# Attention and a feed-forward layer on one core: reciprocals and mixed tails go through the two PV banks

## The chip, the core and the metric

The kernel runs on one core of a Trainium2 chip. The metric is the device time of one execution in microseconds. Engines are named as in the profile: PE (TensorE), DVE (VectorE), ACT (ScalarE), POOL (GpSimd), SP (the DMA queue's engine).

## The reference, cut to what matters

```python
def _attn_ref(q, k, v, w1, b1, w2):          # q, k, v: (4, 8, 576, 64)
    scores = scale * np.matmul(q, k.transpose(0, 1, 3, 2))
    ...                                      # bias: a small network of relative positions
    scores = scores + bias.transpose(2, 0, 1)[None, :, :, :]
    scores = scores - np.max(scores, axis=-1, keepdims=True)
    attn = np.exp(scores)
    attn = attn / (np.sum(attn, axis=-1, keepdims=True) + 1e-09)
    return np.matmul(attn, v)

def _moe_ref(x, w_in, w_out):                # x: (2304, 512), d_ff = 2048
    h = x @ w_in
    g = np.maximum(0.01 * h, h)
    return g @ w_out
```

The output of attention, with heads side by side, is the x of the feed-forward layer.

## The kernel before, in words

Three parts follow each other. The bias is generated first (to about 49 us), then attention runs, then the feed-forward part (from 314.68 us). The order of all instructions is written out by hand, each engine runs its own in that order, and the framework only adds waits. It orders accesses of different engines to one PSUM bank of a tile.

Attention works on 16 units. A unit is a pair of heads of one batch entry. It has nine score tiles, in the order A0, B0, A1, B1, M, A2, B2, A3, B3 (`KINDS`). A and B are the two heads, 128 query rows each; M is the mixed tile, the last 64 rows of both heads. `step(n)` handles tile n of 144:

- `qk_mm(n)` (L242 for M, L249 for the others): the score product of tile n on PE, into a ring tile.
- `softmax_a(n)` (L272): the score read on DVE, which adds the bias, writes p and takes the row's extreme.
- `recip(n-1)` if that was M or B3 (L288, L289 on DVE, L292 and L294 on POOL): reciprocals of the row sums, spread to a tile rb.
- `pv_exit` for a PV group that is done (L363, DVE): the PV result times the transposed reciprocals (slot 8 of `PT`), into x.
- `transposes(n-3)` (PE, L305): tile n-3 is transposed into another ring tile by 64x64 blocks, 8 to 16 products, and copied to `PT` by ACT (L342, for M L326). For M the tails of the mixed tile, its reciprocals and those of group 0 go into the same ring tile, which DVE copies out in three more instructions (L329 twice, L312). For B3 the reciprocals of group 1 do so, copied by L312.
- `pv` (L357): PV products of the queue `pv_q` that are due. A unit has two groups: group 0 for the query rows of A0, B0, A1, B1 and half of M, group 1 for the rest. Each group has five parts c, of four PE instructions in the trace. Group 0 comes whole two steps after M's transposes, that is in the step of the next unit's A0. Group 1 comes two steps after B3's transposes (c = 0, 1, 2; M's step) and four steps after (c = 3, 4; B2's step).
- `softmax_b` (L280): exp on ACT.

In steps of A0, M and B3 two conversion instructions for the feed-forward weights follow on DVE (L417 to L423).

PSUM has eight banks. Ring tiles take six: two buffers `s` of two banks and one buffer `u` of two, in turn s, s, u (`sttile`). A step takes two ring tiles, first for the score product, then for the transposes; 18 turns make a unit, so each kind falls on the same tag in every unit. M's and A3's score products use u, and so do the transposes of B3, A1 and A2. M's transposes use s; that buffer is next used by the score product of the following A0. The buffer u with B3's transposes is next used by the score product of M. The last two banks are two buffers `o`, one for each PV group in turn.

Of the kernel before, what the change touches and what calls it, by code (L numbers as in the profile page):

```python
# [8 lines left out]
F32 = mybir.dt.float32  # L9
# [5 lines left out]
B, H, S, D, HID = 4, 8, 576, 64, 32  # L15
DM, DFF = 512, 2048
NT = B * S
HP = H // 2
# [19 lines left out]
LAG = 3  # L38
# [4 lines left out]
def attention_ffn(ctx: ExitStack, tc: tile.TileContext, qk_in, v_in, wi, wo, cst, out):  # L43
    nc = tc.nc
    PS = bass.MemoryType.PSUM
    xp = ctx.enter_context(tc.tile_pool(name="xp", bufs=1))
    ps = ctx.enter_context(tc.tile_pool(name="ps", bufs=2, space=PS))
    po = [ExitStack()]
# [12 lines left out]
    def po_open():  # L61
        po[0].close()
        po[1:] = [po[0].enter_context(tc.tile_pool(name="po", bufs=2, space=PS, reuse_waits="tile"))]

    def pstile(tag):
        shape = [128, 512] if tag in "to" else [128, 1024]
        return (ps if tag == "s" else po[1]).tile(shape, F32, tag=tag, name="ps_" + tag, bufs=1 if tag == "u" else 2)

    turns = [0]

# [10 lines left out]
    PT = ap.tile([128, 2, 10, HS], F32, name="PT")  # L81
# [170 lines left out]
    mx_t, sm_t, rb_t, pair = {}, {}, {}, [None]  # L252
# [43 lines left out]
    outs = {}  # L296
    pv_q = []

    def banks(t, a, b):
        return t[:].rearrange("p (r x) -> p r x", r=2)[:, :, a:b]  # L300

    def turn(dst, src):
        for r in range(2):
            q = slice(64 * r, 64 * r + 64)
            nc.tensor.transpose(dst[:, r, :], src[q, :], ident[q, q])  # L305

    def turn_rb(t, rb):
        for i in range(2):
            turn(t[:, :, 64 * i:64 * i + 64], rb[:, 128 * i:128 * i + 128])

    def copy_rb(u, g, t):
        nc.vector.tensor_copy(PT[:, g, 8, 0:256].rearrange("p (i r c) -> p i r c", i=2, r=2), t.rearrange("p r (i c) -> p i r c", i=2))  # L312

    def transposes(n, at):
        u, kind = tile_id(n)
        p = pp.pop(n)
        p0 = S + 64 if kind[0] == "B" else 0
        t0 = sttile()
        for jb in range(4):
            turn(banks(t0, 64 * jb, 64 * jb + 64), p[:, p0 + 128 * jb:p0 + 128 * jb + 128])  # L320
        if kind == "M":
            rb = rb_t.pop((u, 0))
            turn(banks(t0, 320, 384), p[:, 512:640])
            turn(banks(t0, 256, 320), rb[:, 256:384])
            turn_rb(banks(t0, 384, 512), rb)
            nc.scalar.copy(out=PT[:, :, 0:8, 256:288].rearrange("p g (j h) c -> p g j h c", h=2), in_=banks(t0, 0, 256).rearrange("p h (j g c) -> p g j h c", j=4, g=2))  # L326
            for h in range(2):
                r = slice(64 * h, 64 * h + 64)
                nc.vector.tensor_copy(PT[r, :, 8:10, 256:288], banks(t0, 256, 384)[r, h, :].rearrange("p (a g c) -> p g a c", a=2, g=2))  # L329
            copy_rb(u, 0, banks(t0, 384, 512))  # L330
            pv_q.extend((at, u, 0, c) for c in range(5))
            return
        ic, h = int(kind[1]), 0 if kind[0] == "A" else 1
        g, i2 = ic // 2, ic % 2
        c = slice(128 * i2, 128 * i2 + 128)
        nj = 4 + h
        if h == 1:
            turn(banks(t0, 256, 320), p[:, 512:640])
        if kind == "B3":
            turn_rb(banks(t0, 320, 448), rb_t.pop((u, 1)))  # L340
        dst = PT[:, g, :, c].rearrange("p (j h) c -> p j h c", h=2)[:, 0:nj, h, :]
        nc.scalar.copy(out=dst.rearrange("p j (r c) -> p j r c", r=2), in_=banks(t0, 0, 64 * nj).rearrange("p r (j c) -> p j r c", j=nj))  # L342
        if kind == "B3":
            copy_rb(u, 1, banks(t0, 320, 448))
            pv_q.extend((at + 2 * (c > 2), u, 1, c) for c in range(5))

    pv_out = []

    def pv():
        _, u, g, jb = pv_q.pop(0)  # L350
        hp, b = divmod(u, B)
        if jb == 0:
            outs[u, g] = pstile("s" if (u, g) == (HP * B - 1, 1) else "o")
        o, pt = outs[u, g], PT[:, g]
        for h in range(2):
            l, r = vv[u][:, jb, 64 * h:64 * h + 64], pt[:, 2 * jb + h if jb < 4 else 9, :]
            nc.tensor.matmul(o[64 * h:64 * h + 64, 0:HS], l, r, start=(jb == 0), stop=(jb == 4))  # L357
        if jb == 4:
            pv_out.append((hp, S * b + HS * g, o, pt[:, 8, :]))

    def pv_exit():
        hp, t0, o, r = pv_out.pop(0)
        nc.vector.tensor_mul(x1[hp][:, t0:t0 + HS], o[:, 0:HS], r)  # L363

    NTILE = 9 * HP * B

    def step(n):
        first = n == 7
        if first:
            transposes(n - LAG, n + 1)  # L370
        if n == 5:
            recip(n - 1)
        if 1 < n < NTILE:
            qk_mm(n)
            if n % 9 == 4 and n // 9 + 2 < HP * B:
                load_unit(n // 9 + 2)
            if 10 <= n < 10 + LATE:
                dst, e = late[n - 10]
                nc.sync.dma_start(out=dst, in_=e)
            softmax_a(n)  # L380
        if n != 5 and 0 <= n - 1 < NTILE and KINDS[(n - 1) % 9] in ("M", "B3"):
            recip(n - 1)
        while pv_out and n < NTILE + LAG + 2:
            pv_exit()
        if 0 <= n - LAG < NTILE and not first:
            transposes(n - LAG, n + 2)
        while pv_q and pv_q[0][0] <= n:
            pv()
        while ex_q and n != 5:
            softmax_b()  # L390
# [209 lines left out]
    with tc.manual_schedule():  # L600
# [6 lines left out]
        for n in range(NTILE + LAG + 6):  # L607
            u, i = divmod(n, 9)
            if u == 0:
                while done < GEN_AT[i]:  # L610
                    gen_tick(done)
                    done += 1
            if n == 9:
                gen.close()
                early = pools["early"] = ctx.enter_context(tc.tile_pool(name="early", bufs=1, side="right"))
                w1b[0] = w1b[1] = early.tile([128, 2, 7, 256], F32R, name="w1a")
                for m in range(EARLY + 1):
                    y2[m] = early.tile([128, DM], F32, name=f"y2_{m}")
                early.tile([128, 24], F32, name="gap")
                r_last = early.tile([128, 320], F32, name="r_last")  # L620
                for c in ("raw", "y1"):
                    pools[c] = ctx.enter_context(tc.tile_pool(name=c, bufs=1, side="right"))
            if n == 2:
                po_open()
            step(n)
            if n == 13:
                w_fill()
                early_ops = conversion(halves_[:NE])
                for g in range(PRE):
                    t = 9 * (4 + 3 * g)  # L630
                    extra[t + 1] = [(s_sum, g, 0)]
                    extra[t + 4] = [(s_sum, g, 1), (s_sum, g, 2)]
                    extra[t + 6] = [(w1_hi, g, 0, nc.gpsimd.tensor_copy)]
                    extra[t + 7] = [(w1_hi, g, 1)]
                    extra[t + 10] = [(s_sum, g, 3)]
                    extra[t + 12] = [(w1_hi, g, 3)]
                    extra[t + 13] = [(w1_lo, g, 0, nc.gpsimd), (w1_lo, g, 1, nc.gpsimd)]
                    extra[t + 15] = [(w1_hi, g, 4, nc.gpsimd.tensor_copy)]
                    extra[t + 17] = [(w1_out, g, 0)]
                    extra[t + 18] = [(w1_out, g, 1)]  # L640
                    extra[t + 19] = [(w1_lo, g, 3, nc.gpsimd)]
                    extra[t + 22] = [(w1_lo, g, 4, nc.gpsimd)]
                    extra[t + 24] = [(w1_out, g, 2)]
                    extra[t + 26] = [(w1_out, g, 3)]
                extra[9 * 14 + 4] = [(w1_in, 0)]
                for k, o in enumerate((3, 2, 4)):
                    extra[NTILE - 8 + (0, 1, 5)[k]] = [(x_sum, 0, o)]
            for f, *args in extra.get(n, ()):
                f(*args)
            left = {0: 2, 4: 2, 8: 2}.get(i, 0) if n >= 18 else 0  # L650
            while early_ops and left:
                f, *args = early_ops.pop(0)
                f(*args)
                left -= f == w_bits
            if u < HP * B:
                if u % B == B - 1 and u // B + 1 < HP:
                    c = {1: "0", 2: "1", 4: "2", 5: "M", 6: "3"}.get(i)
                    if c:
                        load_bias(u // B + 1, c)
                if i == 8 and u + 2 < HP * B:  # L660
                    load_v(u + 2)
# [194 lines left out]
```

## Time and profile before

| | us |
|---|---|
| median of three runs | 696.05 (695.57 to 696.22) |
| profiled execution | 696.33 |
| its span | 694.5 |

Shares of that span in which an engine was busy: PE 95%, PE's weight loads 72%, DVE 65%, ACT 60%, POOL 19%.

In the rows of the profile, a line such as L357 is that line of the kernel before; `PE ps_o L357` means PE writing the tile ps_o there. An idle time in brackets is the time in which the engine had nothing to run just ahead of the row, with what ended it by the trace. PE's instructions overlap: a group's duration runs to the end of its last one, and the next group can start before that, so the time that a group costs is read from start to start.

### The profile page before, as it was taken

Reading aid. Unit: us, or ns where it says so; the run is one execution under the profiler, and the core shown is the slowest. Engines: PE = TensorE matmul, PEld = TensorE weight load, DVE = VectorE, ACT = ScalarE, POOL = GpSimd, SP = SyncE. Lnnn points to the kernel's source line nnn. Section 1 sums busy time; section 2 is a strip of 40 time slices with the busy share of each in tenths; the row PEclk is TensorE's granted clock in tenths of the full one; section 3 lists DMA queues with packets and bytes.
Section 4 is the critical chain, followed back from the end, with each engine's and each line's share of the span. In section 5 each row is a group of like instructions: output and inputs, shape, how many; then the busy total and the mean of one; then the engine's idle time right before and its main releaser. Section 6 shows DMA issues by size and latency. Waiting matters only on the chain.

```text
span 694.5 us, 13060 instructions
## 1 busy us (share of the span) xinstructions
PE 657.4 (95%) x4990; PEld 498.5 (72%) x4990; DVE 454.7 (65%) x1041; ACT 417.6 (60%) x879; POOL 131.0 (19%) x177
## 2 busy tenths in 40 slices
PE   9987899989988999989999999999999999999997
PEld 5434555555555555558889889899889889898886
DVE  7994677776777777659899987534343663334343
ACT  8996788888888888777445546433333544333332
POOL 0000002322222220133000051221114421221110
PEclk9999999999999999999999999999999999999999
DMA  8989247447654783025256526452222244432302
GB/s 276 300 280 325 74 132 258 160 139 272 211 192 152 241 282 147 6 107 197 92 170 201 213 65 235 176 198 108 107 107 106 107 168 164 152 138 107 107 1 91
DMA packets 36542, 113.95 MB, mean 164 GB/s; under 512 B 7584, under 2 KB 12320, under 8 KB 34048
## 3 DMA queue, kind: packets, MB, share of 16 engines
q1 hardware_dynamic: 36272, 112.91, 47.7%
q8 instruction: 39, 0.64, 0.4%
q14 instruction: 23, 0.19, 0.1%
q10 hardware_dynamic: 208, 0.21, 0.1%
HBM read 82.59 MB, written 30.52 MB: 163 GB/s over the span
## 4 chain that ended last, share of the span: by engine, by line
PE 83%; ACT 10%; DVE 3%; issue 1%; DMA 1%; POOL 0%; POOLq 0%; ACTq 0%
PE ps_t L532 25%; PE ps_s L574 19%; PE ps_o L357 12%; PE ps_o L574 10%; PE ps_s L305 5%; ACT p L280 4%; ACT PT L342 4%; PE ps_s L249 3%; PE ps_u L249 3%; DVE p L272 2%; PE ps_u L242 2%; PE ps_o L145 1%; PE ps_t L145 1%; DVE PT L312 1%; PE ps_s L145 1%
## 5 line engine op out<-in xcount | busy, mean ns | idle before, releaser
L544 DVE TENSOR_TENSOR c<-ps_t,c 128x384 f32<-128x384 f32 x164 | 88.8, 555 | 128.9 <-PE ps_t L532 127.8
L551 ACT ACTIVATE g<-c 128x384 fp32r<-128x384 f32 x96 | 50.6, 527 | 179.7 <-DVE c L544 154.6
L574 PE MATMUL ps_s<-ws,g 128*128 128x512 f32 x576 | 148.3, 393 | 0.0
L574 PEld LDWEIGHTS ps_s<-ws,g 128*128 128x128 f32 x576 | 106.7, 188 | 16.9
L280 ACT ACTIVATE p<-p,mx 128x576 f32<-128x576 f32 x128 | 99.5, 778 | 13.2 <-DVE mx L272 11.0
L532 PE MATMUL ps_t<-xo,w1c 128*128 128x384 f32 x504 | 99.2, 335 | 0.1
L532 PEld LDWEIGHTS ps_t<-xo,w1c 128*128 128x128 f32 x504 | 89.7, 188 | 6.7 <-DVE c L544 0.4
L532 PE MATMUL ps_t<-xo,w1a 128*128 128x384 f32 x474 | 93.5, 335 | 0.0
L532 PEld LDWEIGHTS ps_t<-xo,w1a 128*128 128x128 f32 x474 | 84.3, 188 | 6.3 <-DVE xo L521 0.4
L357 PE MATMUL ps_o<-PT,v 128*64 128x288 f32 x620 | 87.0, 420 | 0.0
L249 PE MATMUL ps_s<-raw 64*128 64x288 f32 x388 | 70.0, 437 | 15.6 <-ACT PT L342 11.2
L272 DVE CUSTOM_DVE_ANT_0 p<-ps_s,bias 128x576 f32<-128x576 f32 x97 | 72.1, 746 | 18.8 <-PE ps_s L249 18.8
L482 POOL TENSOR_TENSOR ws<-y,ws 128x512 fp32r<-128x512 f32 x34 | 45.3, 1334 | 184.1 <-PE ps_t L532 147.3
L574 PE MATMUL ps_o<-ws,g 128*128 128x512 f32 x288 | 74.0, 393 | 0.0
L557 DVE TENSOR_TENSOR g<-gf,g 128x384 fp32r<-128x384 f32 x95 | 61.0, 642 | 14.4 <-ACT gf L552 14.2
L342 ACT COPY PT<-ps_s 128x640 f32<-128x640 f32 (+1 forms) x80 | 50.9, 636 | 22.3 <-PE ps_s L305 22.3
L574 PEld LDWEIGHTS ps_o<-ws,g 128*128 128x128 f32 x288 | 53.4, 188 | 8.5
L357 PEld LDWEIGHTS ps_o<-PT,v 128*64 128x64 f32 x620 | 41.1, 138 | 25.3 <-issue 1.3
L305 PEld LDWEIGHTS ps_s<-ident,p 64*128 64x128 f32 x736 | 30.6, 138 | 30.7 <-DVE mx L272 26.0
L249 PEld LDWEIGHTS ps_s<-raw 64*128 64x128 f32 x388 | 30.3, 188 | 26.6 <-ACT PT L342 14.2
L552 ACT ACTIVATE gf<-c 128x384 f32<-128x384 f32 x96 | 49.1, 511 | 0.0
L272 DVE CUSTOM_DVE_ANT_0 p<-ps_u,bias 128x576 f32<-128x576 f32 x31 | 23.5, 757 | 34.7 <-PE ps_u L249 33.7
(128 smaller groups left out, 834.9 us busy)
## 6 DMA issues: line engine op xcount, KB each, us to landing
w1a<-w SPq DMA_DIRECT2D x10, 1792.0 KB, 7.5
w1c<-w SPq DMA_DIRECT2D x9, 1792.0 KB, 7.4
raw<-qk_in SPq DMA_DIRECT2D x16, 896.0 KB, 6.7
w<-w1a SPq DMA_DIRECT2D x20, 448.0 KB, 5.0
bias<-scr SPq DMA_DIRECT2D x16, 512.0 KB, 5.7
raw<-wi SPq DMA_DIRECT2D x16, 512.0 KB, 3.9
raw<-wo SPq DMA_DIRECT2D x16, 512.0 KB, 4.0
scr<-x SPq DMA_DIRECT2D x24, 295.5 KB, 4.3
```

Of the source, the lines that this page charges most:

```text
L249: nc.tensor.matmul(s_[:, S0 + HS * hh:S0 + HS * hh + HS], q_[r, c:c + 128], k_[r, HS * h:HS * h + HS], start=True, stop=True)
L272: nc.vector.tensor_tensor_reduce(out=p, in0=s_[:, S0:S0 + S], in1=bt, scale=-0.125, scalar=3.4e38, op0=ALU.add, op1=ALU.min, accum_out=i)
L280: nc.scalar.activation(out=p, in_=p, func=AF.Exp, bias=i, scale=-1.0, accum_out=sm)
L305: nc.tensor.transpose(dst[:, r, :], src[q, :], ident[q, q])
L342: nc.scalar.copy(out=dst.rearrange("p j (r c) -> p j r c", r=2), in_=banks(t0, 0, 64 * nj).rearrange("p r (j c) -> p j r c", j=nj))
L357: nc.tensor.matmul(o[64 * h:64 * h + 64, 0:HS], l, r, start=(jb == 0), stop=(jb == 4))
L532: nc.tensor.matmul(o, w[:, a, PROD[j], c], x[:, b, k, :], start=(n == 0), stop=(n == 5))
L544: nc.vector.tensor_add(a if c == src else c_new(g, c), bank[g, j], a)
L551: nc.scalar.activation(out=t[:, 0], in_=h, func=AF.Prelu, alpha=0.01)
L552: nc.scalar.activation(out=gf[g, c][:], in_=h, func=AF.Prelu, alpha=0.01)
L557: eng.tensor_sub(t[:, 1], gf.pop((g, c))[:], t[:, 0].bitcast(F32))
L574: nc.tensor.matmul(o, t[:, a, c], w[:, b], start=(m == 0 and n == 0), stop=(m == NG - 1 and n == 5))
```

## The change

Four edits:

- A tile `oo` of two banks takes the place of the two `o` buffers, is allocated once as attention starts, and lasts to its end. Bank 0 takes PV of group 0, bank 1 that of group 1 (in the last unit group 1 still uses a ring tile).
- The mixed tail, the mixed reciprocals and the reciprocals of both groups are transposed into `oo` (columns 0 to 127 and 320 to 447 of both banks) instead of the ring tile; the three DVE copies read them there. The ring tile of M and of B3 is then read by ACT alone.
- Both PV groups come in two parts: c = 0, 1 one step after the transposes, c = 2, 3, 4 three steps after. Group 0 is then in the steps of B3 and of the next unit's B0, group 1 in those of B1 and A2.
- The exits of PV groups stand at the head of a step, ahead of the score product and its read on DVE.

```diff
--- before.py
+++ after.py
@@ -64,7 +64,7 @@
 
     def pstile(tag):
         shape = [128, 512] if tag in "to" else [128, 1024]
-        return (ps if tag == "s" else po[1]).tile(shape, F32, tag=tag, name="ps_" + tag, bufs=1 if tag == "u" else 2)
+        return (ps if tag == "s" else po[1]).tile(shape, F32, tag=tag, name="ps_" + tag, bufs=1 if tag in ("u", "oo") else 2)
 
     turns = [0]
 
@@ -304,12 +304,14 @@
             q = slice(64 * r, 64 * r + 64)
             nc.tensor.transpose(dst[:, r, :], src[q, :], ident[q, q])
 
-    def turn_rb(t, rb):
+    oo = []
+
+    def turn_rb(u, g, rb):
         for i in range(2):
-            turn(t[:, :, 64 * i:64 * i + 64], rb[:, 128 * i:128 * i + 128])
-
-    def copy_rb(u, g, t):
-        nc.vector.tensor_copy(PT[:, g, 8, 0:256].rearrange("p (i r c) -> p i r c", i=2, r=2), t.rearrange("p r (i c) -> p i r c", i=2))
+            turn(banks(oo[0], 64 * i, 64 * i + 64), rb[:, 128 * i:128 * i + 128])
+
+    def copy_rb(u, g):
+        nc.vector.tensor_copy(PT[:, g, 8, 0:256].rearrange("p (i r c) -> p i r c", i=2, r=2), banks(oo[0], 0, 128).rearrange("p r (i c) -> p i r c", i=2))
 
     def transposes(n, at):
         u, kind = tile_id(n)
@@ -320,15 +322,15 @@
             turn(banks(t0, 64 * jb, 64 * jb + 64), p[:, p0 + 128 * jb:p0 + 128 * jb + 128])
         if kind == "M":
             rb = rb_t.pop((u, 0))
-            turn(banks(t0, 320, 384), p[:, 512:640])
-            turn(banks(t0, 256, 320), rb[:, 256:384])
-            turn_rb(banks(t0, 384, 512), rb)
+            turn(banks(oo[0], 384, 448), p[:, 512:640])
+            turn(banks(oo[0], 320, 384), rb[:, 256:384])
+            turn_rb(u, 0, rb)
             nc.scalar.copy(out=PT[:, :, 0:8, 256:288].rearrange("p g (j h) c -> p g j h c", h=2), in_=banks(t0, 0, 256).rearrange("p h (j g c) -> p g j h c", j=4, g=2))
             for h in range(2):
                 r = slice(64 * h, 64 * h + 64)
-                nc.vector.tensor_copy(PT[r, :, 8:10, 256:288], banks(t0, 256, 384)[r, h, :].rearrange("p (a g c) -> p g a c", a=2, g=2))
-            copy_rb(u, 0, banks(t0, 384, 512))
-            pv_q.extend((at, u, 0, c) for c in range(5))
+                nc.vector.tensor_copy(PT[r, :, 8:10, 256:288], banks(oo[0], 320, 448)[r, h, :].rearrange("p (a g c) -> p g a c", a=2, g=2))
+            copy_rb(u, 0)
+            pv_q.extend((at + 2 * (c > 1), u, 0, c) for c in range(5))
             return
         ic, h = int(kind[1]), 0 if kind[0] == "A" else 1
         g, i2 = ic // 2, ic % 2
@@ -337,12 +339,12 @@
         if h == 1:
             turn(banks(t0, 256, 320), p[:, 512:640])
         if kind == "B3":
-            turn_rb(banks(t0, 320, 448), rb_t.pop((u, 1)))
+            turn_rb(u, 1, rb_t.pop((u, 1)))
         dst = PT[:, g, :, c].rearrange("p (j h) c -> p j h c", h=2)[:, 0:nj, h, :]
         nc.scalar.copy(out=dst.rearrange("p j (r c) -> p j r c", r=2), in_=banks(t0, 0, 64 * nj).rearrange("p r (j c) -> p j r c", j=nj))
         if kind == "B3":
-            copy_rb(u, 1, banks(t0, 320, 448))
-            pv_q.extend((at + 2 * (c > 2), u, 1, c) for c in range(5))
+            copy_rb(u, 1)
+            pv_q.extend((at + 2 * (c > 1), u, 1, c) for c in range(5))
 
     pv_out = []
 
@@ -350,7 +352,7 @@
         _, u, g, jb = pv_q.pop(0)
         hp, b = divmod(u, B)
         if jb == 0:
-            outs[u, g] = pstile("s" if (u, g) == (HP * B - 1, 1) else "o")
+            outs[u, g] = pstile("s") if (u, g) == (HP * B - 1, 1) else oo[0][:, 512 * g:512 * g + 512]
         o, pt = outs[u, g], PT[:, g]
         for h in range(2):
             l, r = vv[u][:, jb, 64 * h:64 * h + 64], pt[:, 2 * jb + h if jb < 4 else 9, :]
@@ -370,6 +372,8 @@
             transposes(n - LAG, n + 1)
         if n == 5:
             recip(n - 1)
+        while pv_out and n < NTILE + LAG + 2:
+            pv_exit()
         if 1 < n < NTILE:
             qk_mm(n)
             if n % 9 == 4 and n // 9 + 2 < HP * B:
@@ -380,10 +384,8 @@
             softmax_a(n)
         if n != 5 and 0 <= n - 1 < NTILE and KINDS[(n - 1) % 9] in ("M", "B3"):
             recip(n - 1)
-        while pv_out and n < NTILE + LAG + 2:
-            pv_exit()
         if 0 <= n - LAG < NTILE and not first:
-            transposes(n - LAG, n + 2)
+            transposes(n - LAG, n + 1)
         while pv_q and pv_q[0][0] <= n:
             pv()
         while ex_q and n != 5:
@@ -622,6 +624,7 @@
                     pools[c] = ctx.enter_context(tc.tile_pool(name=c, bufs=1, side="right"))
             if n == 2:
                 po_open()
+                oo.append(pstile("oo"))
             step(n)
             if n == 13:
                 w_fill()
```

## Rows read from the trace of the kernel before

**Rows 1.** The page: engines' shares of the span; one group by line (count, busy, mean).

```profile
PE 657.4 (95%) x4990; PEld 498.5 (72%) x4990; DVE 454.7 (65%) x1041; ACT 417.6 (60%) x879; POOL 131.0 (19%) x177
...
L342 ACT COPY PT<-ps_s 128x640 f32<-128x640 f32 (+1 forms) x80 | 50.9, 636 | 22.3 <-PE ps_s L305 22.3
```

**Rows 2.** Sums by stretch: length, busy per engine (instructions), granted clock, DMA share, GB/s.

```profile
62.00:64.60 2.60, 2.60 (x12) 0.98 (x8) 0.00 (x0) 0.70 (x2) 0.00 (x0) 0.52 1.01 352
69.53:85.85 16.32, 14.63 (x172) 8.75 (x172) 10.12 (x31) 12.82 (x29) 1.28 (x4) 1.00 0.24 79
85.85:298.19 212.34, 190.28 (x2236) 113.88 (x2237) 157.48 (x439) 173.33 (x376) 49.71 (x84) 1.00 0.54 179
...
314.68:694.50 379.82, 376.04 (x1873) 337.26 (x1872) 223.29 (x393) 159.51 (x319) 72.56 (x72) 1.00 0.39 138
```

**Rows 3.** Waits of PE, 60 to 300 us: sum in us, times, longest.

```profile
PE ps_s L249 <- ACT PT L342: 10.9, 10, 1.1
PE ps_u L242 <- DVE PT L312: 6.6, 15, 0.5
```

**Rows 4.** PE in order of time, one unit: start, duration, instruction, count, idle before.

```profile
134.85 0.72 PE L242 MATMUL ps_u<-raw 64*64 64x288 f32 x8 [0.43 <-DVE PT L312]
135.52 0.53 PE L305 MATMUL ps_s<-ident,p 64*128 64x64 f32 x10
135.98 1.68 PE L357 MATMUL ps_o<-PT,v 128*64 128x288 f32 x12
137.59 0.76 PE L249 MATMUL ps_s<-raw 64*128 64x288 f32 x4
138.18 0.41 PE L305 MATMUL ps_u<-ident,p 64*128 64x64 f32 x8
138.42 0.71 PE L249 MATMUL ps_s<-raw 64*128 64x288 f32 x4
...
139.67 1.19 PE L357 MATMUL ps_o<-PT,v 128*64 128x288 f32 x8
140.79 0.76 PE L249 MATMUL ps_u<-raw 64*128 64x288 f32 x4
141.38 0.47 PE L305 MATMUL ps_s<-ident,pM 64*128 64x64 f32 x10
...
141.87 0.71 PE L249 MATMUL ps_s<-raw 64*128 64x288 f32 x4
142.41 0.46 PE L305 MATMUL ps_u<-ident,p 64*128 64x64 f32 x8
143.96 0.76 PE L249 MATMUL ps_s<-raw 64*128 64x288 f32 x4 [1.09 <-ACT p L280]
...
145.04 2.65 PE L357 MATMUL ps_o<-PT,v 128*64 128x288 f32 x20
...
148.45 0.70 PE L249 MATMUL ps_s<-raw 64*128 64x288 f32 x4
```

**Rows 5.** DVE in order of time, the same unit.

```profile
135.74 0.76 DVE L272 CUSTOM_DVE_ANT_0 pM<-ps_u,biasM 128x576 f32<-128x576 f32 x1 [0.28 <-PE ps_u L242]
...
141.59 0.76 DVE L272 CUSTOM_DVE_ANT_0 p<-ps_u,bias 128x576 f32<-128x576 f32 x1 [1.49 <-PE ps_u L249]
...
142.28 0.45 DVE L363 TENSOR_TENSOR x<-ps_o,PT 128x288 f32<-128x288 f32 x1
142.83 0.59 DVE L329 COPY PT<-ps_s 64x128 f32<-64x128 f32 x2
143.44 0.43 DVE L312 COPY PT<-ps_s 128x256 f32<-128x256 f32 x1
...
150.71 0.42 DVE L312 COPY PT<-ps_u 128x256 f32<-128x256 f32 x1 [0.47 <-ACT PT L342]
```

**Rows 6.** PE in order of time, in unit 0.

```profile
59.96 0.47 PE L305 MATMUL ps_u<-ident,p 64*128 64x64 f32 x8 [2.39 <-DVE PT L312]
60.36 4.33 PE L357 MATMUL ps_o<-PT,v 128*64 128x288 f32 x20
```

## The prediction, made before the changed kernel was run

> **What bounds the kernel now.** I read the page's first table, then the sums by stretch, then who TensorE (PE) waits for, then one unit in order of time on PE and on VectorE (DVE). The reader is to see four things.
>
> PE is busy 95% of the span [rows 1]. The stretches differ: from 314.68 us (the feed-forward part) PE has 376.04 of 379.82 us, so whatever attention saves before it comes off the end. In attention PE has 190.28 of 212.34 us, with VectorE at 157.48 and ScalarE (ACT) at 173.33: no engine is full, and waits between them set the pace [rows 2].
>
> A unit is nine score tiles. From the mixed product of unit 1 at 69.53 to that of unit 15 at 298.19, two edges of the stretches [rows 2], 14 units take 228.66 us, 16.33 each. PE's named waits are two per unit: 1.09 us ahead of A0's score product (143.96) and 0.43 ahead of the mixed one (134.85) [rows 3, 4].
>
> Both are waits for a PSUM ring tile. The second is put down to the copy of B3's reciprocals (L312), which itself starts 0.47 us late, behind ACT's copy out of the same tile [rows 5]. The first is put down to ACT [rows 3, 4], but VectorE shows who it is: exit 142.28 to 142.73, two tail copies, then the reciprocal copy L312 from 143.44 to 143.87, and PE goes on 0.09 later [rows 4, 5]. That tile is the one with M's transposes; three DVE copies keep it after ACT has read it.
>
> **The change part by part.** Durations: a score product takes 0.59 to the next work behind PV (140.79 to 141.38), 0.54 behind transposes (141.87 to 142.41). Eight transposes that needn't wait take 0.24 (138.18 to 138.42), so ten 0.30; the sixteen of M 0.49 (141.38 to 141.87). Ten that were held, with the switch to PV behind them, 0.46 (135.52 to 135.98), so eight 0.40. PV of 8 takes 1.12 (139.67 to 140.79), of 12 1.61 (135.98 to 137.59), of 20 2.65 [rows 4]. From the start of a product to the end of its score read: 1.56 (140.79 to 141.59 + 0.76), the mixed one 1.65 (134.85 to 135.74 + 0.76); the next product or transposes in that ring tile start 0.06 later (142.35 to 142.41). The three copies take 1.04 (142.83 to 143.87), one exit 0.45 [rows 4, 5], a copy of ACT out of a ring tile 0.64 [rows 1].
>
> Nothing is removed: instructions of each kind and their shapes stay. PV's three batches per unit (20, 12, 8) become four (8, 12, 8, 12), one more switch: 5.46 against 5.38. No DMA, no POOL work and no ACT instruction is moved; SP's and POOL's queues keep their order. What moves is when tiles come free and what fills the holes. I walk a unit in two stretches, each from a product's start.
>
> From A3's product to A1's, before: 140.79 to 148.45, 7.66 [rows 4]. After:
> A3's product 0 to 0.54. M's transposes need the tile of B2's score, whose read ends at about 0.67 (B2's product starts 0.89 ahead): 0.73 to 1.27, the last eight into the lasting tile. B3's product to 1.81. A2's transposes with the switch to 2.15; A3's score read has ended at 1.56.
> Then the first PV part, and here the change adds a wait: PV's banks now hold the reciprocals and tails, so PV stands behind the three DVE copies. They follow A3's read at 1.56, end at 2.60 and release PE at 2.69. PE waits 0.54, with the next product and through it DVE and ACT queued behind.
> PV of 8 to 3.81; A0's product to 4.40 (M's ring tile is read by ACT alone now, and free at about 2); B2's transposes to 4.70; B0's product to 5.24; A3's transposes need A0's read (3.81 + 1.56 + 0.06 = 5.43) and go with the switch to 5.83; PV of 12 to 7.44. Gain 0.22: the wait of 1.09 comes back as 0.54, a hold of 0.2 and the extra switch.
>
> From A1's product to the next A3's, before: 16.33 - 7.66 = 8.67. After:
> A1's product to 0.59; B3's ten transposes to 0.89 (they need B0's read; before, B0's product stood behind 20 PV products that ran to 147.69, right ahead of A1's at 148.45 [rows 4]; now it starts 2.74 ahead); four more into the lasting tile to 1.01, for which the exit must have read bank 0: it starts as PV ends and takes 0.45. B1's product to 1.55. A0's transposes wait for A1's read (1.56 + 0.06) and go to 2.02.
> PV of 8 needs the copy of the reciprocals: it follows A1's read, 1.56 + 0.43 + 0.09 = 2.08. Done 3.20.
> The mixed product starts at once (its tile was freed by ACT at about 1.8): the 0.43 wait is covered by PV. To 3.80; B0's transposes 4.10; A2's product 4.64; A1's transposes wait for the mixed read (3.20 + 1.65 + 0.06 = 4.91), to 5.31; PV of 12 to 6.92; B2's product 7.51; B1's transposes 7.81. Gain 0.86.
>
> A unit after: 7.44 + 7.81 = 15.25, gain 1.08. Over the 14 units that is 15.1 us.
>
> The exits ahead of the score read cost nothing: an exit waits for the PV that ended the step before, and the read behind it waits for a product that PE starts only after that PV; exit 0.45 is over before the read's 0.80 (140.79 to 141.59). Without that cover it would cost 0.45 twice a unit. What it buys is in the first stretch: the three copies no longer stand behind an exit [rows 5].
>
> Unit 0 is apart. There PE sat 2.39 us for L312 (59.96), and the 20 PV products behind it took 4.33 instead of 2.65, at a granted clock of 0.52 (62 to 64.6), the 1.2 GHz level [rows 2, 6]. After, the transposes there wait for ACT's copy only, 1.1 earlier (the three copies). An idle time of about 1.3 remains; the 1.09 in each later unit left the granted clock at 1.00 [rows 2, 4], and 1.3 is nearer to that than to 2.39, so I take the clock as kept: 1.7 more. Bounds: 0 and 1.7. The tail after 298.19 runs out of score products to fill holes with; I count half a unit's gain, 0.5, bounds 0 and 1.1.
>
> A rule of the notes against the rows. L312 sits idle 0.47 behind ACT's copy out of the same tile, though the two read different columns; where it follows other DVE copies (143.44) it doesn't wait [rows 5]. If it is the tile's banks that hold it, the 0.47 goes, as ACT then reads another tile. If not, it would still come after ACT's copy, and PV's part in B1's step about 0.2 later: 3 us in all, 680.6. I take the former. The Trainium skill, "PSUM — Partial Sum Buffer", section "PSUM bank collisions raise a hardware error", says that two engines on one bank must be kept apart by semaphore, two reads too, whatever the columns. By that rule the 0.47 is a matter of banks; but it also speaks against this change, since PV and the copies, which had banks of their own, now have to take turns, the 0.54 of the first stretch.
>
> Sum: 15.1 + 1.1 + 1.7 + 0.5 = 18.4. The profiled execution took 696.33 (span 694.5); the median of the runs shown is 0.28 lower, 696.05. 696.05 - 18.4 = 677.6.
>
> **The rivals.** (a) The new wait is as long as the old one. Against the walk speaks that VectorE is 74% busy in attention [rows 2] and the mixed reciprocals come through POOL: if the three copies end 0.6 later, PE waits 1.1 ahead of PV in B3's step. The 14 units then give 0.5 each, 7, with 1.1 and 0.5 around them: 687.5. For the walk: no conversion work is issued between A3's read and these copies.
> (b) Slower: PE, in order, stands at PV while the product that would feed DVE and ACT is queued behind. Place: B3's step. Price: if a pair of conversion instructions (1.4, an estimate: two reads of 0.76 less their overlap) stood ahead of the copies, the wait would be 1.9 in place of 1.09 and 0.43, and the rest of the second stretch's gain would be lost behind it: 0.4 a unit longer, 5.5 in all, 701.5. It decides once that wait is over 1.5, the copies 1.0 later than in my walk. Against it: the pairs are issued at the ends of A0's, M's and B3's steps, so DVE would have to be over two steps behind; its waits for PE products (1.49 at 141.59 [rows 5]) say that it is ahead.
> (c) The change doesn't do what it says, as the wait of 1.09 belongs to ACT after all. Then little is lost: PV of 8 now runs where that wait was. 681.
> (d) More: the 0.54 goes because copies start as soon as their transposes land. 14.75 a unit, 670.5.
>
> **How the numbers follow.** The forecast with (c) and (d) in its neighbourhood 0.78, (a) 0.15, (b) 0.05, something that eats all of it 0.02. The bounds: the new wait between 0 and 1.1 is 7.5 down and 7.8 up; clock and tail 2.2 up. Range 671 to 687.5. Faster by over 0.2% 0.92, within 0.2% (about what a measurement of this kernel can tell from no change) 0.03, slower 0.05.
>
> **What would show it.** Right: the distance of the mixed products at about 15.25; no PE wait ahead of A0's and the mixed products; instead waits of about 0.5 ahead of PV, released by L312; the exits starting as PV ends; a granted clock of 1.00 from 60 to 65 us; the feed-forward part as long as before. Wrong: PE waits at PV over 1 us, or score reads that start late because an exit is ahead of them, or new waits for DMA landings as attention gets shorter.

## The result and the profile after

The changed kernel takes 675.32 us (median of four runs, 674.75 to 675.59), the kernel before beside it 695.81. The ratio is 0.9707, 95% interval 0.969 to 0.9723: 2.9% faster. The profiled execution of the changed kernel has a span of 672.9 us, 21.6 less than before.

Where it went is read from four edges in both traces: the mixed product of unit 1, that of unit 15, and the first product of the feed-forward part.

| stretch | before, us | after, us | saved | forecast |
|---|---|---|---|---|
| start to the mixed product of unit 1 | 69.53 | 66.41 | 3.1 | 2.8 |
| to that of unit 15 (14 units) | 228.66 | 212.08 | 16.6 | 15.1 |
| to the first feed-forward product | 16.49 | 14.59 | 1.9 | 0.5 |
| to the end | 379.82 | 379.82 | 0.0 | 0.0 |

The first and third rows need a second look. Ahead of the mixed product of unit 1 PE has done 28 PV products in the changed kernel and 20 in the kernel before, as group 1's first part now comes in B1's step (141.45 in the rows below) and not behind the mixed product (135.98 in [rows 4]). Those eight take 1.12 us, and after the mixed product of unit 15 they are missing in the same way, 52 in place of 60. With the same work in each row, the start saved 4.2 us and the stretch behind unit 15's mixed product 0.8.

The two profiled executions also differ in their granted clock (last section): about 1.7 of the 21.6 us is that, and the medians are 20.5 apart.

A steady unit lasts 15.10 us (127.47 to 142.57, below) where 15.25 were forecast and 16.33 had been; unit 1, the first of the fourteen, takes 15.77.

The sums by stretch of the changed kernel, to lay beside [rows 2]; columns are the stretch, its length, busy time of PE, its weight loads, DVE, ACT and POOL, granted clock, DMA share and GB/s:

```profile
62.00:64.60 2.60, 2.60 (x34) 1.67 (x30) 1.15 (x4) 1.67 (x6) 0.00 (x0) 1.00 0.95 357
66.41:82.18 15.77, 14.91 (x175) 8.82 (x173) 10.22 (x30) 12.46 (x29) 1.28 (x4) 1.00 0.33 119
82.18:278.49 196.31, 190.60 (x2238) 113.37 (x2237) 158.11 (x438) 171.44 (x377) 50.40 (x84) 1.00 0.57 194
293.08:672.90 379.82, 376.04 (x1873) 337.26 (x1872) 222.98 (x393) 159.13 (x319) 72.41 (x72) 1.00 0.39 138
```

PE does the same work in attention (190.60 us busy, 190.28 before) in 16.0 us less: 97% busy in place of 90%. The feed-forward part has the same length to 0.01 us, so all that attention saved came off the end.

PE in order of time, one unit of the changed kernel, to lay beside [rows 4] (L359 is PV, L305 transposes, L249 and L242 score products):

```profile
127.47 0.71 PE L242 MATMUL ps_u<-raw 64*64 64x288 f32 x8
...
131.78 0.47 PE L305 MATMUL ps_s<-ident,p 64*128 64x64 f32 x10
132.08 0.71 PE L249 MATMUL ps_u<-raw 64*128 64x288 f32 x4
132.82 0.46 PE L305 MATMUL ps_s<-ident,pM 64*128 64x64 f32 x8
133.11 0.23 PE L305 MATMUL ps_oo<-ident,pM 64*128 64x64 f32 x2
133.17 0.35 PE L305 MATMUL ps_oo<-ident,rb 64*128 64x64 f32 x6
133.36 0.70 PE L249 MATMUL ps_s<-raw 64*128 64x288 f32 x4
133.90 0.40 PE L305 MATMUL ps_u<-ident,p 64*128 64x64 f32 x8
134.70 1.19 PE L359 MATMUL ps_oo<-PT,v 128*64 128x288 f32 x8 [0.39 <-issue]
135.82 0.76 PE L249 MATMUL ps_s<-raw 64*128 64x288 f32 x4
...
137.83 1.68 PE L359 MATMUL ps_oo<-PT,v 128*64 128x288 f32 x12
139.44 0.76 PE L249 MATMUL ps_s<-raw 64*128 64x288 f32 x4
...
141.06 0.46 PE L305 MATMUL ps_s<-ident,p 64*128 64x64 f32 x8
141.45 1.19 PE L359 MATMUL ps_oo<-PT,v 128*64 128x288 f32 x8
142.57 0.72 PE L242 MATMUL ps_u<-raw 64*64 64x288 f32 x8
```

Both waits of before are gone: A0's product (135.82) and the mixed one (142.57) start right behind PV. One wait is new, 0.39 ahead of PV's first part in B3's step (134.70). The trace calls it "issue", that is, it names nobody.

That the wait ahead of A0's product belonged to the DVE copies and not to ACT can be read in the kernel before: ACT's copy out of M's ring tile was over at 142.67, 1.29 us ahead of A0's product at 143.96.

```profile
142.08 0.59 ACT L326 COPY PT<-ps_s 128x512 f32<-128x512 f32 x1 [0.59 <-PE ps_s L305]
```

DVE in the same unit, to lay beside [rows 5] (L365 the exit, L331 and L314 the copies out of the lasting tile), and the ACT copy that runs beside the last of them:

```profile
132.84 0.76 DVE L272 CUSTOM_DVE_ANT_0 p<-ps_u,bias 128x576 f32<-128x576 f32 x1
...
133.57 0.59 DVE L331 COPY PT<-ps_oo 64x128 f32<-64x128 f32 x2
134.17 0.42 DVE L314 COPY PT<-ps_oo 128x256 f32<-128x256 f32 x1
...
139.56 0.46 DVE L365 TENSOR_TENSOR x<-ps_oo,PT 128x288 f32<-128x288 f32 x1 [0.36 <-PE ps_oo L359]
140.24 0.76 DVE L272 CUSTOM_DVE_ANT_0 p<-ps_s,bias 128x576 f32<-128x576 f32 x1 [0.23 <-PE ps_s L249]
...
140.93 0.42 DVE L314 COPY PT<-ps_oo 128x256 f32<-128x256 f32 x1
```

```profile
140.54 0.69 ACT L344 COPY PT<-ps_u 128x640 f32<-128x640 f32 x1 [0.43 <-PE ps_u L305]
```

The exit (139.56 to 140.02) lies between the end of PV and the read of A1's score, and the read still waits 0.23 for its product: the exit is covered, as the walk has it. The copy of B3's reciprocals starts at 140.93, right behind the read, while ACT is still copying (140.54 to 141.23). The 0.47 that L312 had stood behind ACT in [rows 5] is gone.

### The profile page after: what moved, and what is told of

It reads as the page before. It is cut to its first block, busy times and chain, and to the rows that moved or that the text cites. A ratio compares the mean times of both kernels' runs of the same rounds, so it can differ in the third digit from the quotient of the medians.

```text
span 672.9 us, 13094 instructions
## 1 busy us (share of the span) xinstructions
PE 656.1 (97%) x4990; PEld 497.4 (74%) x4990; DVE 455.3 (68%) x1041; ACT 414.7 (62%) x879; POOL 131.5 (20%) x177
## 4 chain that ended last, share of the span: by engine, by line
PE 90%; ACT 3%; DVE 3%; issue 2%; DMA 1%; ACTq 0%; DVEq 0%
PE ps_t L534 25%; PE ps_s L576 20%; PE ps_oo L359 12%; PE ps_o L576 10%; PE ps_s L249 8%; PE ps_s L305 5%; PE ps_u L305 2%; PE ps_u L249 2%; DVE r L134 2%; PE ps_u L242 1%; PE ps_oo L305 1%; ACT p L280 1%; ACT r L132 1%; ACT x L152 1%; PE ps_o L145 1%
## 5 line engine op out<-in xcount | busy, mean ns | idle before, releaser
L359 PE MATMUL ps_oo<-PT,v 128*64 128x288 f32 x620 | 88.9, 415 | 5.8 <-issue 5.8
L249 PE MATMUL ps_s<-raw 64*128 64x288 f32 x388 | 70.7, 442 | 0.9 <-ACT PT L344 0.9
L359 PEld LDWEIGHTS ps_oo<-PT,v 128*64 128x64 f32 x620 | 40.3, 136 | 28.2 <-ACT PT L328 7.5
L305 PEld LDWEIGHTS ps_s<-ident,p 64*128 64x128 f32 x736 | 31.6, 138 | 26.5 <-DVE mx L272 13.9
L249 PEld LDWEIGHTS ps_s<-raw 64*128 64x128 f32 x388 | 29.7, 187 | 22.8 <-issue 14.8
L134 DVE TENSOR_SCALAR r<-cs,bps 128x304 f32<-128x304 f32 (+17 forms) x117 | 42.1, 434 | 0.1
```

Of the source, the lines that this page charges most:

```text
L134: nc.vector.tensor_scalar(out=t[:, :w], in0=ltw[:, :w], scalar1=bps[:, k:k + 1], scalar2=0.0, op0=ALU.add, op1=ALU.max)
L249: nc.tensor.matmul(s_[:, S0 + HS * hh:S0 + HS * hh + HS], q_[r, c:c + 128], k_[r, HS * h:HS * h + HS], start=True, stop=True)
```

## The experiments

The change has three parts that can be had alone: the lasting tile (T), PV's new steps (P), the exits at the head of a step (E). All eight combinations were run; "unit" is the distance of mixed products in the steady part of each trace. Times are medians, in which executions at two granted clocks are mixed; for the kernel before that is worth some 1.5 us (last section). The units are free of it, since every unit from unit 1 on ran at full clock in every trace.

| | exits behind the read | exits first (E) |
|---|---|---|
| two PV buffers, old steps | 695.9, unit 16.33 (before) | 693.84, unit 16.19 (e4) |
| P | 681.22, unit 15.41, 15.14 and 15.68 in turn (e2) | 681.15, unit 15.41, in turn likewise (e7) |
| T | 694.2, unit 16.45 (e1) | 676.5, unit 15.28 (e6) |
| T and P | 694.57, unit 16.43 (e3) | 675.32, unit 15.10 (the change) |

### The exits behind the read again (e3)

```diff
-        while pv_out and n < NTILE + LAG + 2:      # head of the step
-            pv_exit()
         if 1 < n < NTILE:
             qk_mm(n)
...
+        while pv_out and n < NTILE + LAG + 2:
+            pv_exit()
         if 0 <= n - LAG < NTILE and not first:
```

> The changed kernel with one edit undone: the exits stand again behind the score read. Theory (the lasting tile makes the exit part of PE's loop: B3's four reciprocal transposes wait for the exit of group 0, so an exit behind the score read holds PE until that read is over): PE waits about 1.0 us in A1's step ahead of those transposes (read ends 1.56 after the product, exit 0.45, against 0.9 at which PE gets there), a unit goes to 16.2 to 16.5, the time to 692 to 698. Rival (the exits' place is worth only their own 0.45 on DVE ahead of M's copies): at most 0.45 a unit, 675 to 682.

694.57 us, ratio to the kernel before 0.9987 (0.9978 to 0.9997): nearly the whole gain is lost. PE in A1's step of this kernel, and DVE there:

```profile
130.32 0.47 PE L305 MATMUL ps_u<-ident,p 64*128 64x64 f32 x10
131.82 0.34 PE L305 MATMUL ps_oo<-ident,rb 64*128 64x64 f32 x4 [1.02 <-DVE x L365]
```

```profile
130.53 0.76 DVE L272 CUSTOM_DVE_ANT_0 p<-ps_s,bias 128x576 f32<-128x576 f32 x1 [0.51 <-PE ps_s L249]
131.22 0.08 DVE L272 DVE_READ_ACCUMULATOR2_ANT mx<- 128x1 f32 x1
131.22 0.45 DVE L365 TENSOR_TENSOR x<-ps_oo,PT 128x288 f32<-128x288 f32 x1
```

B3's reciprocals go into banks that the exit of group 0 has still to read. With the exit behind the score read, PE stands 1.02 us until 131.82, 0.15 after the exit ends (131.67). The theory holds and the rival (0.45 at most) falls: in the lasting tile the exit is a link of PE's chain. The unit is 16.43, 1.33 more than in the change; 1.02 of it is this wait.

### PV in its old steps (e6)

```diff
-            pv_q.extend((at + 2 * (c > 1), u, 0, c) for c in range(5))
+            pv_q.extend((at + 1, u, 0, c) for c in range(5))
...
-            pv_q.extend((at + 2 * (c > 1), u, 1, c) for c in range(5))
+            pv_q.extend((at + 1 + 2 * (c > 2), u, 1, c) for c in range(5))
```

> The changed kernel with PV in its old steps and batches (20, 12, 8). Theory (the freed ring tiles pay; PV's new steps only fill holes that are then small): a unit of 15.2 to 15.4, 677 to 680. Rival (spreading PV pays, since 20 PV products in one step keep B0's product back): the hold of B3's transposes and of A0's product returns, 15.8 or more a unit, 685 to 690.

676.5 us, ratio 0.973 (0.9713 to 0.9747). The unit is 15.28; the theory holds, just under its range of times. With tile and exits in place PV's new steps are worth 0.18 a unit and 1.2 us between the medians (1.8 between the two profiled executions, both at full clock). PE in A0's step:

```profile
134.60 0.71 PE L249 MATMUL ps_s<-raw 64*128 64x288 f32 x4
135.92 0.52 PE L305 MATMUL ps_s<-ident,p 64*128 64x64 f32 x10 [0.61 <-DVE mx L272]
```

A0's product (134.60) doesn't wait here, though no PV stands ahead of it: with M's ring tile free of the DVE copies, the wait of 1.09 is gone. One hold of A0's step is left: B2's transposes sit 0.61 for a score read, with 20 PV products behind them.

### The two PV buffers with PV's new steps (e7, e2) and the exits alone (e4)

e7 is the kernel before with these lines and the exits at the head of a step, e2 the same without the move of the exits, e4 the kernel before with that move alone (the diff of e3 read from below):

```diff
-            pv_q.extend((at, u, 0, c) for c in range(5))
+            pv_q.extend((at + 2 * (c > 1), u, 0, c) for c in range(5))
...
-            pv_q.extend((at + 2 * (c > 2), u, 1, c) for c in range(5))
+            pv_q.extend((at + 2 * (c > 1), u, 1, c) for c in range(5))
...
-            transposes(n - LAG, n + 2)
+            transposes(n - LAG, n + 1)
```

> Without the lasting tile: the kernel before (two PV buffers, reciprocals and tails in the ring tile) with PV's new steps and the exits at the head of a step. Theory: the ring tiles stay held by the DVE copies, but PV of 8 now runs where PE waited for them, so more than half of the gain is there: 15.3 to 15.6 a unit, 680 to 685. Rival (only freeing the ring tiles pays): 16.0 or more a unit, 690 to 696.

681.15 us, ratio 0.9797 (0.9778 to 0.9817).

> PV's new steps alone, in the kernel before: two PV buffers, reciprocals in the ring tile, exits behind the score read. Theory: PV fills the two waits, 15.3 to 15.7 a unit, 680 to 686. Rival (the ring tiles must be freed first): 16.0 or more, 690 to 696.

681.22 us, ratio 0.979 (0.9776 to 0.9805). PE in the steps of B3 to B0 of e2, and the first of the three copies on DVE:

```profile
137.69 0.42 PE L305 MATMUL ps_u<-ident,p 64*128 64x64 f32 x8
138.07 1.19 PE L357 MATMUL ps_o<-PT,v 128*64 128x288 f32 x8
139.19 0.76 PE L249 MATMUL ps_s<-raw 64*128 64x288 f32 x4
139.81 0.53 PE L305 MATMUL ps_s<-ident,p 64*128 64x64 f32 x10
140.17 0.70 PE L249 MATMUL ps_u<-raw 64*128 64x288 f32 x4
141.81 0.46 PE L305 MATMUL ps_s<-ident,p 64*128 64x64 f32 x8 [0.94 <-DVE mx L272]
```

```profile
138.05 0.59 DVE L329 COPY PT<-ps_s 64x128 f32<-64x128 f32 x2 [0.46 <-ACT PT L326]
```

M's ring tile is still held until the three copies are over (139.08 in this unit), yet A0's product starts at 139.19, since PV of 8 runs where PE had sat. So PV's new steps give seven tenths of the gain (14.7 us) with no tile freed. What stays is the 0.94 at 141.81: the copies wait 0.46 for ACT's copy out of the same tile (138.05), so A0's read and with it A3's transposes are late. In the next unit this wait is 0.41, and so on in turn, 0.67 on average; the changed kernel has its 0.39 in place of it, by size 0.28 of the 0.31 by which its unit is shorter. The theory of both runs holds; the rival, that only freed ring tiles pay, falls.

> The kernel before with one edit: the exits at the head of a step. Theory: the three copies of M's step come 0.1 to 0.45 earlier and with them the end of the 1.09 wait; 0.1 to 0.4 a unit, 690 to 694.5. Rival (the exits block DVE at the head of a step while PV is still running, and score reads come late): slower, 697 or more.

693.84 us, ratio 0.9972 (0.996 to 0.9984): 0.14 a unit, as the wait of 1.09 is 0.94 now.

```profile
141.41 0.76 PE L249 MATMUL ps_s<-raw 64*128 64x288 f32 x4 [0.94 <-ACT p L280]
```

The theory holds. The rival, DVE blocked at the head of a step, falls.

### The lasting tile alone (e1)

The edits of e3 and e6 together, in the changed kernel.

> The lasting tile alone: the kernel before with reciprocals and tails in it, PV in its old steps, exits behind the score read. Theory (the tile needs the exits ahead of the read: M's transposes into it wait for group 1's exit, which stands behind A3's read in that very step): the wait of 1.09 is exchanged for one of about the same length, 16.2 to 16.5 a unit, 691 to 697 (unit 0 alone gives some 3). Rival (freeing the ring tiles pays by itself): 15.3, 677 to 681.

694.2 us, ratio 0.9977 (0.9968 to 0.9987), and the steady unit, 16.45, is longer than before; what it gains is ahead of unit 1. PE in A3's step:

```profile
137.34 0.41 PE L305 MATMUL ps_s<-ident,pM 64*128 64x64 f32 x8
138.83 0.28 PE L305 MATMUL ps_oo<-ident,pM 64*128 64x64 f32 x2 [1.09 <-DVE x L365]
```

The wait of 1.09 has moved from A0's product to M's transposes: they stand for group 1's exit, which stands behind A3's read. The rival (freeing the ring tiles pays by itself) falls.

### M's reciprocals copied twice (e8)

```diff
             copy_rb(u, 0)
+            copy_rb(u, 0)
```

> The changed kernel with the copy of M's reciprocals (0.43 on DVE) done twice. Theory (PV's first part in B3's step stands behind the last of those copies, and PE in order behind it): the wait there grows from 0.39 to about 0.75, 0.3 to 0.4 a unit, 680 to 681.5. Rival (the wait of 0.39 belongs to something else, such as ACT's copy of M or PE's own queue): the copy is hidden on DVE, 675 to 677.

682.13 us, ratio 0.9803 (0.9788 to 0.9817); the unit is 15.56. PE and DVE in B3's step:

```profile
137.01 1.19 PE L360 MATMUL ps_oo<-PT,v 128*64 128x288 f32 x8 [0.85 <-ACT p L280]
```

```profile
136.03 0.88 DVE L314 COPY PT<-ps_oo 128x256 f32<-128x256 f32 x2
```

0.46 more on DVE is 0.46 more wait (0.85 for 0.39) and 0.46 more in the unit. PV starts 0.10 after the last copy ends (136.91), as in the changed kernel (134.59 to 134.70, 0.11). So the wait that the trace gives to "issue" there and to an exp on ACT here belongs to the copies. The size was a little over the forecast: all of the added copy shows, nothing of it is hidden.

### PV where no part waits for the copies (e5)

```diff
-            pv_q.extend((at + 2 * (c > 1), u, 0, c) for c in range(5))
+            pv_q.extend((at + 1 + (c > 1), u, 0, c) for c in range(5))
...
-            pv_q.extend((at + 2 * (c > 1), u, 1, c) for c in range(5))
+            pv_q.extend((at + 2, u, 1, c) for c in range(5))
```

> The changed kernel with PV moved so that no part waits for M's copies: group 0 in the steps of A0 (c = 0, 1) and B0 (the rest), group 1 whole in B1's step plus one, that is M's. Theory (the wait of 0.4 ahead of PV in B3's step is the last one that costs, and one switch goes): 14.8 to 15.0 a unit, 670.5 to 673.5. Rival (without PV in B3's and B1's steps the products of A0 and M wait for their ring tiles or for reads again): 15.3 or more, 678 or more.

671.79 us, ratio to the kernel before 0.966 (0.9644 to 0.9676), 0.5% less than the changed kernel. PE from B3's product to PV's first part in A0's step:

```profile
132.36 0.71 PE L249 MATMUL ps_s<-raw 64*128 64x288 f32 x4
132.90 0.41 PE L305 MATMUL ps_u<-ident,p 64*128 64x64 f32 x8
133.27 0.76 PE L249 MATMUL ps_s<-raw 64*128 64x288 f32 x4
134.32 0.52 PE L305 MATMUL ps_s<-ident,p 64*128 64x64 f32 x10 [0.29 <-DVE mx L272]
134.77 1.19 PE L359 MATMUL ps_oo<-PT,v 128*64 128x288 f32 x8
```

A0's product runs while DVE copies, and PV comes when the copies are long over. The wait of 0.39 goes; 0.29 of it comes back ahead of B2's transposes, for B3's score read, which stands behind those copies on DVE. The unit is 14.94. This is the best version that was run.

### The start of attention (e9)

```diff
                 po_open()
+                pstile("o"), pstile("o")
             step(n)
```

> The kernel before with one edit: the two PV buffers are allocated, unused, as attention starts, so that the ring buffer u falls on the other two banks, as it does in the changed kernel where the lasting tile is allocated first. Theory (the changed kernel starts attention's first u product earlier because those banks were emptied by an earlier eviction of the bias): u's first product moves from 49.2 to about 48 us and the first mixed product from 50.85 to 50 or less, 0.5 to 1 us off the time at most. Rival (those are differences from execution to execution): the first mixed product at 50.6 to 51.1 as before, no difference.

695.74 us, ratio 1.0003 (0.9993 to 1.0012): no difference, so the theory falls as to the time. The trace moves as the theory has it (first mixed product at 49.84, in the kernel before 50.85, in the changed one 49.81), so the rival's own sign, 50.6 to 51.1, falls too. Most of the gain is taken back at once:

```profile
47.94 0.76 PE L249 MATMUL ps_u<-raw 64*128 64x288 f32 x4 [0.38 <-ACT x L154]
...
55.12 0.52 PE L305 MATMUL ps_s<-ident,p 64*128 64x64 f32 x10 [1.42 <-DVE mx L272]
```

At 55.12 it is 0.38 ahead of the kernel before (55.50), and the mixed product of unit 1 is at 69.06, 0.47 ahead; 0.27 of that is PV of 20 at 4.06 us in place of 4.33, a matter of the clock. So which banks `u` falls on is worth 0.2 to 0.4 in these traces, which is also what executions differ by: e5 is the same program as the change up to there and has its first mixed product at 50.49, 0.68 later.

## Why the prediction was right

**What bounds attention: right.** Waits between engines did, two per unit, and the feed-forward part passed all of it on.

**The walk of a unit: right, by 0.15.** Set from A3's product as zero, the first stretch reads, forecast against trace: M's transposes 0.73 and 0.74, B3's product 1.27 and 1.28, PV of 8 at 2.69 and 2.62, A0's product 3.81 and 3.74, PV of 12 at 5.83 and 5.75, A1's product 7.44 and 7.36. The 0.08 of this stretch is in one term: the new wait, 0.54 forecast, 0.39 measured. A3's product came behind transposes here, so its read ended 1.52 after its start and not 1.56, and the three copies and the step to PE took 1.10 and not 1.13; PE for its part was there at 2.23 and not at 2.15. In the second stretch (7.74, forecast 7.81) A0's transposes go at 1.62 as forecast, and PV of 8 follows at 2.01 (2.08 forecast), with no idle time in the trace. The copy of the reciprocals ends 0.10 ahead of it (141.35 against 141.45), as the copies do in B3's step, so what holds it there, the copy or PE's own transposes, can't be told. One price of the prediction is off: it takes PV of 20 at its duration, 2.65, where the next product starts 2.58 behind it (145.04 to 147.62), so the extra switch costs 0.15 and not 0.08; the walk doesn't use it.

**The new wait: right in place and cause.** It is PV behind the three copies (e8), with the whole queue of PE behind it: a copy more is 0.46 us a unit.

**The rule on banks: right, as far as the waits show it.** The copy of the reciprocals (L312, now L314) doesn't wait for ACT once the two read different tiles (140.93 against 140.54 to 141.23). That shows how the framework orders the two; no run here let two engines use one bank without a wait. That PV and the copies must take turns in their common banks is the price, 0.39 a unit, and e3 and e1 show a second one that the prediction had only as a condition.

**The exits: free, as forecast, but worth more than forecast.** That they cost nothing ahead of the read is borne out (the read waits 0.23 for its product behind the exit). What their place buys was sized too low: the prediction named that the three copies no longer stand behind an exit, 0.45 at most. e3 puts the exits back and a unit costs 1.33 more, since an exit behind a read is late by the read too, and PE waits for it. The prediction's own line on the four reciprocal transposes "for which the exit must have read bank 0" held the link; it wasn't followed to what it costs when it breaks. "Without that cover it would cost 0.45 twice a unit" is another case, an exit that delays a read; no run has it.

**Which part pays: shown otherwise than told.** The prediction said that what moves is when tiles come free and what fills the holes. The runs weigh the two: filling the holes with PV alone gives 14.7 us (e2), the lasting tile alone nothing in a steady unit (e1), because its exits then hold PE. With the exits first it gives 17.3 (e6 against e4). So the gains don't add: with tile and exits in place PV's new steps are worth 1.2 (e6). Both answer the same two waits, one by ending them, one by working through them.

**Unit 0 and the tail: the tail right, unit 0 too low.** With the eight PV products put back, the tail saved 0.8 (0.5 forecast, bounds 0 and 1.1): two waits there, of 1.13 and 0.24, became two of 0.39 and 0.20. Unit 0 saved 4.2 where 2.8 were forecast. Of this the idle time gives 1.15 (2.39 to 1.24; 1.1 forecast) and the clock 1.7 (PV of 20 at 4.33 in place of 2.65), both as forecast for these two executions. The other 1.4 the prediction didn't count: 0.7 stands ahead of the idle time (55.50 against 54.83) and 0.7 behind it, up to unit 1's mixed product, where the kernel before has waits of 0.31 and 0.53. The first 0.7 is no more than executions of one program differ by (e9). So the 21.6 of the two profiled executions is 18.4 and 1.5 from the units, 1.4 from unit 0 and 0.3 from the tail.

**The clock: right for the profiled execution, and in part luck.** The other three runs of the changed kernel have a mean granted clock of 0.997 (last section). Between runs at the same clock the change saves 19.9 to 20.8 us, and the sum without its clock term is 16.7. That term covered about half of what was counted too low elsewhere, so 677.6 against 675.32 is closer than its other terms earned.

**The rivals.** (a) is out: the wait is 0.39, though e8 shows its slope, and 0.7 us more would have brought it about. (b) is out for the change, but e1 shows that kind of loop: a unit longer than before when an exit stands behind a read. (c) is out: ACT was done with the tile 1.29 us before the wait ended, and in e6, where the DVE copies no longer read that tile, the wait is gone. That e2 and e7, in which the copies still hold the tile, come to its 681 (681.2) is no proof of its mechanism: what they keep is a wait ahead of A3's transposes. (d) didn't happen, as the wait is there; e5 comes near its 670.5 by another way.

## What to carry to other kernels

Where an in-order engine sits at a buffer, see first whether work that is ready can be issued into that hole: here that took a change of three numbers and gave seven tenths of the gain. A tile that two uses share makes every reader of it a link of the writer's chain: list those readers and put each ahead of anything that it needn't wait for, as the tile and the exits' place were worth 19 us together and about 2 each alone. A walk through one period in rows of the trace, engine by engine, with each hold looked up in the queue that ends it, came within 1% of the unit here. And where two stretches of two traces are compared, see whether the same work lies between their edges.

## What the runs showed of the hardware

The granted clock after the idle time of unit 0 is not one value. Five traces have the idle of 2.4 us there: in four PV or the products behind it then run at 0.50 of the full clock, the 1.2 GHz level, for some microseconds (before, e2, e7, e9), in one, e4, they don't, and 20 PV products take 2.65 us there instead of 4.33. The same stretch of e4:

```profile
60.00:62.00 2.00, 2.00 (x22) 1.23 (x19) 0.90 (x4) 1.69 (x4) 0.00 (x0) 1.00 0.94 278
62.00:64.60 2.60, 2.58 (x36) 1.45 (x30) 1.55 (x6) 1.25 (x4) 0.00 (x1) 1.00 1.02 327
```

Six traces have an idle of about 1.2 us in its place (the change, e1, e3, e5, e6, e8), and in all of them the clock stays at 1.00 from 60 to 64.6 us. So the 1.7 us that the prediction counted for the clock is right for the pair of profiled executions.

Each run's mean granted clock is on record and goes further. Of 45 runs of the kernel before, 14 have a mean of 1.000 and take 694.1 to 694.8 us; the other 31 have 0.995 to 0.998 and take 695.6 to 696.5. The medians of the two groups are 1.5 us apart, near the 1.7 of the trace. Of the four runs of the changed kernel only the profiled one has 1.000 (674.75 us); three have 0.997 and take 675.3 to 675.6. So a lower clock is a matter of the single execution in both kernels, and no run shows that the change makes it rarer. Where the clock fell in the three runs is not known, as only the profiled one has a trace.
